# Block-sparse attention into a GELU MLP: the first batch in two units instead of three, with GpSimd gathering for the first

## The chip, the cores and the metric

One core of a Trainium2 chip. The metric is the device time of one execution in microseconds (us), as the median of several runs. Engines in the rows of the profile: PE (TensorE matmul), PEld (TensorE weight load), DVE (VectorE), ACT (ScalarE), POOL (GpSimd), SP (SyncE, which here issues DMAs only). A suffix q is an engine's instruction queue.

## The reference

Attention over 768 positions in 24 blocks of 32, in which a block of queries sees its neighbours, the first and the last block and three drawn blocks; the first and last block of queries see everything. The result goes through a two-layer MLP with an exact GELU.

```python
batch, n_heads, seq, head_dim = (4, 8, 768, 64)      # blocks of 32, 3 drawn per block
scores = scale * np.matmul(q, k.transpose(0, 1, 3, 2))
mask = np.abs(blk_i - blk_j) <= 1
mask = mask | (blk_i == 0) | (blk_j == 0) | (blk_i == n_blocks - 1) | (blk_j == n_blocks - 1)
for qb in range(n_blocks):
    for kb in sampled_blocks[qb]:
        mask[qb * block:(qb + 1) * block, kb * block:(kb + 1) * block] = True
scores = np.where(mask, scores, -1000000000.0)
attn = softmax(scores)
x = np.matmul(attn, v)  # heads side by side: 3072 x 512
h = x @ w_in            # 512 x 2048
out = (0.5 * h * (1.0 + erf(h * inv_sqrt2))) @ w_out   # 2048 x 512
```

## The kernel before

Work is cut into **units**. A unit is a batch and a list of "quads", a quad being four blocks of queries (128 tokens). Each batch has a dense part (query blocks 0 and 23, which see all keys) that goes with its first unit, and 22 sparse blocks. Batches 1 to 3 have two units: quads (1, 2, 0) with the dense part, eleven sparse blocks, and quads (3, 4, 5), eleven more. Batch 0 has three: quad 1 with the dense part (four sparse blocks), quads 2 and 0 (seven), and quads 3, 4, 5 (eleven).

`attention` works through a unit's **rounds**: four dense rounds (`d`), then sparse rounds of two blocks (`s`). A round is `scores` (TensorE), `maxima` (VectorE), `exponentials` (ScalarE, line 347 sparse, 351 dense), `turned` (a VectorE transpose, 364 sparse, 369 dense); a group of rounds (a quad) then has `values` (TensorE, 389 dense, 425 sparse), `divided` (VectorE, 440 to 444) and `outputs` (transposes on TensorE at 454, copies on ScalarE at 462 into `xT`). Rounds are software-pipelined by one. The order of all instructions on an engine is written out by hand: `due` says after which round a group is weighed, `hooks` runs extra work after a round, `quota` says how many matmuls of the previous unit's FFN2 (`ffn2_pieces`, line 497) go between rounds. After a unit's attention come its eight FFN1 steps (`ffn1_step`, line 475, GELU at 478), 64 matmuls whose width is 128 columns per quad; a unit's FFN2 fills the attention of the next.

A sparse block's keys and values are gathered into a buffer `gb`: the neighbours, first and last block by `gather_fixed` (VectorE, lines 252 to 259), the three drawn ones by `gather` (line 268), one copy for each drawn block at a place that is read from a register. `block_numbers` (line 208) loads these registers from a list `vf`. VectorE gathers for most blocks and GpSimd for the rest. For batch 0 keys (128 columns) and values (260 columns) are gathered apart, since k arrives before v.

GpSimd issues all loads, in the order of its queue: k, q, v of batch 0, then the four parts of w_in (line 139) and of w_out (144). A load reuses a semaphore of the eighth load before it and waits for that one. `hold_loads` (line 150) is a one-element GpSimd copy that makes the loads behind it wait for some datum. k and q of batch 0 are transposed on TensorE (`turn_heads`, 219) and placed by ScalarE (225, 228); the keys land in `k0`. Those of later batches are loaded by token (111) and transposed by DMA transposes issued on SP (`turn_keys` 118, `turn_queries` 121), and VectorE scales the keys into place (`place_keys`, 125, in `next_keys`). `turn_queries(1)` writes the space of `k0`, so `k0` is first copied to `kvs[0]` (GpSimd, 657). In the first unit batch 1's loads follow its first GELU output; `next_keys(1)` runs in the third unit's attention.

Of the kernel before, what the change touches and what calls it, by code (L numbers as in the profile page):

```python
# [19 lines left out]
def kernel(  # L20
# [142 lines left out]
    load_kq(kn, k, HALVES[0])  # L163
    load_kq(kn, k, HALVES[1])
    zero = const.tile([P, 1], BF16, name="zero")
# [11 lines left out]
    for h in range(H):  # L177
        load_v(0, h)


# [50 lines left out]
    def spaces():  # L231

        views = [psT.tile([P, PI, PP], BF16, name="pt", tag="T")]
        two = psV.tile([P, 2, 1024], BF16, name="pq", tag="V")
        views += [two[:, i, 0:S].rearrange("p (i c) -> p i c", i=PI) for i in range(2)]
        return views + [psO.tile([P, PI, PP], BF16, name="pt", tag="op")]

# [34 lines left out]
    class Unit:  # L272
        def __init__(self, b, quads, dense, i0=0):
# [3 lines left out]
            self.place = {j: i for i, j in enumerate(sorted(self.js), i0)}  # L277
# [243 lines left out]

    def attention(unit, filler, quota, tail, held=0, hooks=None, late=False, ahead=None):

# [3 lines left out]
        rounds = [(unit, rnd) for rnd in unit.rounds[done:]]  # L527
        due = [(max(e - done + 1 + half, held), grp, half) for e, grp in sorted(unit.ends.items())
               for half in range(2)]
        if ahead:  # L530
# [65 lines left out]
    DVE, POOL = mybir.EngineType.DVE, mybir.EngineType.Pool  # L596
    J0, J1 = sorted(units[3].js), units[2].js
    value_list()
    known = block_numbers(units[0].js, DVE)
    first = [psA.tile([P, 2, 1024], BF16, name="pk", tag="A") for _ in range(2)]  # L600
    first = [x[:, i, 0:S].rearrange("p (i c) -> p i c", i=PI) for x in first for i in range(2)]
    first += spaces()
    for i, (which, pr) in enumerate([(w, pr) for w in "kq" for pr in range(NPR)]):
        turn_heads(which, pr, first[i])
        place_heads(which, pr, first[i])
# [10 lines left out]
    def second_values():  # L616

        nc.gpsimd.tensor_copy(mark, sampled(units[0].place[units[0].js[-1]], NR - 1)[0:1, BW - 1:BW])
        gather(units[1], J0[7:], others, KC, BW, nc.gpsimd)
        ones(1)  # L620
# [3 lines left out]
    QUOTAS = {0: ([4, 10, 2, 0, 0], (0, 0, 0)), 1: ([6, 6, 4, 7, 1, 3, 0, 0, 0], (5,))}  # L624

    def more_numbers(js):
        def load():
            for c in range(0, len(js), 6):
                known.update(block_numbers(js[c:c + 6], DVE))
        return load  # L630

# [4 lines left out]
    for n, unit in enumerate(units):  # L636
# [3 lines left out]
        if nxt is not None and not fresh:  # L640
            gather_fixed(k0 if n == 0 else keys(b), nxt.place)
            if n == 0:
                known |= block_numbers(J0[:3], DVE)
                gather(nxt, J0[:3], known, 0, KC)
                gather(nxt, J0[:3], known, KC, BW)
            elif n == 1:
                gather(nxt, J1[:7], known)
            else:
                gather(nxt, J1[:8], known)
        for s in range(KOUT // 2):  # L650
            ffn1_step(n, 2 * s)
            if s == 0:
                if n == 0:
# [3 lines left out]
                    nc.gpsimd.tensor_copy(kvs[0][:, :, 0:KC], k0)  # L657
                    others |= block_numbers(J1[7:], POOL)
                    gather(units[2], J1[7:], others, engine=nc.gpsimd)
                    turn_keys()  # L660
                    turn_queries(1)
                elif fresh and b + 2 < B:
                    xT, t0 = column[b, unit.groups[-2][0]]
                    hold_loads(xT[0:1, 0, t0:t0 + 1])
                    load_by_token(qn, q, b + 2)
                    load_by_token(kn, k, b + 2)
                    turn_queries(b + 2)
                elif nxt is not None and not fresh:
                    if b + 1 < B:
                        if n > 1:  # L670
                            turn_keys()
# [3 lines left out]
                    if n > 1:  # L675
                        gather(nxt, J1[8:], others, engine=nc.gpsimd)
            if s == 7 and nxt is not None:
                table(AF.Exp)
                if n > 1 and not fresh and b + 1 < B:
                    next_keys(b + 1)  # L680
# [7 lines left out]
        if nxt is None:  # L688
            last_output(n)
        elif n == 0:  # L690
            attention(nxt, filler, *QUOTAS[n], hooks={0: [more_numbers(J1[:8])]})
        elif n == 1:
            attention(nxt, filler, *QUOTAS[n], ahead=units[3], hooks={
                0: [more_numbers(J0[7:9])], 1: [lambda: next_keys(1)]})
# [36 lines left out]
```

## Time and profile before

| | before |
|---|---|
| runs, us | 297.98, 301.18, 304.46 (median 301.18) |
| profiled execution, us | 300.21, span 298.4 |
| granted TensorE clock, mean | 0.983 |
| PE / DVE / ACT / POOL busy, us | 254.5 / 212.9 / 208.3 / 113.8 |
| first, second, third FFN1 start, us | 34.84, 56.33, 84.17 |
| first FFN1 of batch 1 and the one after it, us | 117.69, 147.65 |
| loads of batch 1's k start, us | 36.90 |

A row of a timeline or a chain reads: start, busy time, engine, line, operation, output and inputs, shape, count; in brackets the idle time before it and what ended that. The busy time of a group is a sum over its instructions, which may lie apart or overlap. A row of stretches is headed by start:end and gives busy times by engine in that stretch.

### The profile page before, as it was taken

Reading aid. Unit: us, or ns where it says so; the run is one execution under the profiler, and the core shown is the slowest. Engines: PE = TensorE matmul, PEld = TensorE weight load, DVE = VectorE, ACT = ScalarE, POOL = GpSimd, SP = SyncE. Lnnn points to the kernel's source line nnn. Section 1 sums busy time; section 2 is a strip of 40 time slices with the busy share of each in tenths; the row PEclk is TensorE's granted clock in tenths of the full one; section 3 lists DMA queues with packets and bytes.
Section 4 is the critical chain, followed back from the end, with each engine's and each line's share of the span. In section 5 each row is a group of like instructions: output and inputs, shape, how many; then the busy total and the mean of one; then the engine's idle time right before and its main releaser. Section 6 shows DMA issues by size and latency. Waiting matters only on the chain.

```text
span 298.4 us, 11282 instructions
## 1 busy us (share of the span) xinstructions
PE 254.5 (85%) x4775; PEld 147.6 (49%) x4824; DVE 212.9 (71%) x505; ACT 208.3 (70%) x383; POOL 113.8 (38%) x195
## 2 busy tenths in 40 slices
PE   1655795898699799989998899989998999899994
PEld 0523563574455455635553555545554556355644
DVE  7388576689998886769897959588948979682000
ACT  8677277278786885698767966797768856985611
POOL 8747779970089100890396003930030005000000
PEclk9999998599999999999999999999999999999999
DMA  7999999999059911991099215991000110011002
GB/s 105 158 77 202 207 189 158 169 165 66 4 66 153 138 40 47 160 83 46 32 144 167 81 40 117 102 68 41 37 0 2 40 61 16 2 62 50 0 35 75
DMA packets 90630, 25.39 MB, mean 85 GB/s; under 512 B 81745, under 2 KB 87634, under 8 KB 90578
## 3 DMA queue, kind: packets, MB, share of 16 engines
q0 software_dynamic: 68352, 13.64, 81.9%
q1 hardware_dynamic: 22226, 11.01, 15.1%
q8 instruction: 38, 0.62, 0.9%
q14 instruction: 14, 0.11, 0.1%
HBM read 27.26 MB, written 6.29 MB: 112 GB/s over the span
## 4 chain that ended last, share of the span: by engine, by line
PE 57%; ACT 17%; DVE 11%; DMA 7%; issue 4%; DVEq 2%; POOL 1%; POOLq 0%; ACTq 0%
PE hp L475 25%; PE op L497 13%; PE av L425 11%; ACT pp L347 6%; ACT L375 4%; DMA kv<-in_v_dram 4%; DVE nm L330 3%; ACT g L478 3%; DMA qn<-in_q_dram 3%; DVE pT L364 2%; PE tx L454 2%; PE sc L305 2%; PE av L518 2%; PE op L518 2%; DVE xh L444 2%
## 5 line engine op out<-in xcount | busy, mean ns | idle before, releaser
L475 PE MATMUL hp<-xT,w_in_sb 128*128 128x384 bf16 (+2 forms) x576 | 89.0, 318 | 1.7 <-ACT xT L462 1.3
L347 ACT ACTIVATE pp<-sc,nm 128x256 bf16<-128x256 f32 x176 | 75.1, 542 | 9.5 <-DVE nm L330 9.0
L497 PE MATMUL op<-w_out_sb,g 128*128 128x512 bf16 x288 | 75.8, 380 | 4.8 <-issue 3.7
L478 ACT ACTIVATE g<-hp 128x768 bf16<-128x768 f32 (+4 forms) x81 | 53.6, 675 | 34.1 <-PE hp L475 34.0
L475 PEld LDWEIGHTS <-w_in_sb 128*128 128x128 bf16 x576 | 56.6, 103 | 34.5 <-issue 4.1
L330 DVE TENSOR_REDUCE nm<-sc 128x4 f32<-128x1024 f32 (+1 forms) x48 | 53.0, 1110 | 8.3 <-PE sc L305 8.2
L268 DVE COPY gb<-kv 128x388 bf16 (+1 forms) x195 | 45.9, 318 | 0.9 <-issue 0.8
L497 PEld LDWEIGHTS <-g 128*128 128x128 bf16 x336 | 28.3, 97 | 35.2 <-issue 11.4
L268 POOL COPY gb<-kv 128x388 bf16 (+1 forms) x69 | 31.6, 510 | 24.6 <-DVE gb L259 24.2
L425 PEld LDWEIGHTS <-pT 64*32 64x32 bf16 (+1 forms) x2400 | 27.3, 95 | 24.0 <-DVE pT L364 11.9
L364 DVE STREAM_TRANSPOSE pT<-pp 128x512 f32<-128x512 f32 (+1 forms) x48 | 31.5, 656 | 6.5 <-ACT pp L347 4.6
L425 PE MATMUL av<-kv,pT 64*32 64x130 bf16 (+1 forms) x1344 | 29.6, 228 | 7.5 <-DVE pT L364 4.4
L305 PE MATMUL sc<-gb,qT 64*32 64x256 bf16 x704 | 20.0, 280 | 8.7 <-ACT pp L347 4.2
L133 POOL DMA_DIRECT2D kv<-in_v_dram x32 | 25.6, 807 | 1.7 <-DMA qn<-in_q_dram 1.1
L462 ACT COPY xT<-tx 128x192 bf16<-128x192 bf16 (+2 forms) x33 | 13.6, 441 | 17.1 <-PE tx L454 17.1
L305 PEld LDWEIGHTS <-qT 64*32 64x32 bf16 x832 | 11.6, 90 | 26.8 <-issue 20.6
L375 ACT ACT_TABLE_LOAD x17 | 21.8, 1283 | 0.3
L351 ACT ACTIVATE pp<-sc,nm 128x768 bf16<-128x768 f32 x16 | 17.1, 1101 | 6.7 <-DVE nm L333 6.4
L150 POOL COPY mark<-g 1x1 bf16<-1x1 bf16 x4 | 4.1, 1037 | 45.3 <-ACT g L478 45.3
L425 PE MATMUL av<-gb,pT 64*32 64x130 bf16 x1056 | 20.8, 230 | 0.2 <-issue 0.2
L333 DVE TENSOR_REDUCE nm<-sc 128x1 f32<-128x768 f32 x16 | 15.1, 947 | 7.1 <-PE sc L305 6.9
L444 DVE TENSOR_TENSOR xh<-av,rec 128x512 bf16<-128x512 f32 (+2 forms) x28 | 18.3, 652 | 1.0
(65 smaller groups left out, 216.9 us busy)
## 6 DMA issues: line engine op xcount, KB each, us to landing
out_dram<-os SPq DMA_DIRECT2D x23, 256.0 KB, 2.2
kv<-in_v_dram POOLq DMA_DIRECT2D x32, 96.0 KB, 7.0
kn<-in_k_dram POOLq DMA_DIRECT2D x18, 128.0 KB, 5.9
qn<-in_q_dram POOLq DMA_DIRECT2D x18, 128.0 KB, 5.7
w_in_sb<-in_moe_w_in_dram POOLq DMA_DIRECT2D x4, 512.0 KB, 13.4
w_out_sb<-in_moe_w_out_dram POOLq DMA_DIRECT2D x4, 512.0 KB, 17.4
kn<-in_k_dram POOLq DMA_DIRECT2D x2, 384.0 KB, 5.5
qn<-in_q_dram POOLq DMA_DIRECT2D x2, 384.0 KB, 6.9
```

Of the source, the lines that this page charges most:

```text
L133: nc.gpsimd.dma_start(out=kvs[b % 2][32 * hh:32 * hh + 32, 0:NB, c0:c0 + D], in_=v[b, h].rearrange("(n p) d -> p n d", p=BL))
L268: (engine or nc.vector).tensor_copy(sampled(unit.place[j], r)[:, None, c0:c1], src[:, bass.ds(at[j][r], 1), :])
L305: nc.tensor.matmul(o, lhsT=qT[rows, j // 4, pr, BL * (j % 4):BL * (j % 4) + BL], rhs=rhs(rows, pr), start=True, stop=True)
L330: nc.vector.tensor_reduce(out=nm[:, 0:2 * n].rearrange("p (g j) -> p g j", g=2), in_=A4[:, :, 0:n, :], op=ALU.max, axis=AX.X, negate=True)
L347: nc.scalar.activation(at[:, x // n, x % n], A[:, a:a + 256].rearrange("p (e c k) -> p e c k", e=2, k=BL), AF.Exp, bias=nm[:, x:x + 1])
L364: nc.vector.transpose(pt.rearrange("p g c x -> p (g c) x")[:, :, 64 * s:64 * (s + n)].bitcast(F32), pp[:, 0:512 * n].bitcast(F32).rearrang ...
L375: nc.scalar.activation(junk, zero[0:1, 0:1], func)
L425: nc.tensor.matmul(av[32 * s:32 * (s + w), h, V2 * G:V2 * G + V2], lhsT=pv[rows, c % 4, BL * s:BL * (s + w), c // 4], rhs=src[rows], start ...
L444: nc.vector.tensor_tensor(xh[rows, :, 0:m * D].rearrange("p h (x d) -> p h x d", d=D), a[:, :, :, 0:D], rec[rows, :, 0:m, None].to_broadca ...
L475: nc.tensor.matmul(hp[:, i, 0:T], lhsT=w_in_sb[:, ki, (m + i) * P:(m + i + 1) * P], rhs=xTs[n % 2][:, ki, 0:T], start=(ki == 0), stop=(ki ...
L478: nc.scalar.activation(g[:, m + i[0]:m + i[1], 0:T], hp[:, i[0]:i[1], 0:T], AF.Gelu)
L497: nc.tensor.matmul(op, lhsT=g[:, m, t * P:(t + 1) * P], rhs=w_out_sb[:, m, :], start=(m == 0), stop=(m == KOUT - 1))
```

## The change

Batch 0 has two units like the others, so the first unit has four dense rounds and six sparse rounds (eleven blocks) ahead of the first FFN1, which is then 384 columns wide.

- VectorE gathers the keys of the first quad only. GpSimd gathers the keys of the other two quads (21 copies, between its w_in loads) and the values of all three (33 copies, from hooks after rounds 4, 6 and 8), with the w_out loads between them. An explicit list `order` says after which rounds the groups are weighed.
- VectorE loads four lists of block numbers at the start instead of one, GpSimd three.
- `gather_fixed` runs by quad: once at the start, then after rounds 0 and 2.
- The spare blocks of `kvs[1]` are zeroed partly by GpSimd (six of 25), and its ones are written ahead of the weight loads.
- The transposes of k and q go to PSUM tiles that alternate over four pools.
- `k0` is copied to `kvs[0]` by VectorE after the first unit's attention.
- Batch 1's k and q loads still follow the first GELU output, which is now that of the wider first unit; GpSimd's share of the second unit's gather and then batch 1's v follow them. `next_keys(1)` runs after round 2 of the second unit's attention.

```diff
-    nc.scalar.copy(kvs[1][:, :, KC:BW], zero[:, :, None].to_broadcast([P, NB + 1, BW - KC]))
+    nc.scalar.copy(kvs[1][:, 0:FILLED, KC:BW], zero[:, :, None].to_broadcast([P, FILLED, BW - KC]))
...
+    nc.gpsimd.memset(kvs[1][:, FILLED:NB + 1, KC:BW], 0.0)
+    ones(1)
...
-    units = [Unit(0, (1,), True, 9), Unit(0, (2, 0), False), Unit(0, (3, 4, 5), False)]
-    units += [Unit(b, quads, dense) for b in range(1, B)
-              for quads, dense in (((1, 2, 0), True), ((3, 4, 5), False))]
+    units = [Unit(b, quads, dense) for b in range(B)
+             for quads, dense in (((1, 2, 0), True), ((3, 4, 5), False))]
...
-    known = block_numbers(units[0].js, DVE)
+    known = block_numbers(J0[:9], DVE) | block_numbers(J1[:8], DVE)
...
-    gather(units[0], units[0].js, known, 0, KC)
-    gather_fixed(k0, units[0].place)
-    for part in range(4):
-        load_w_in(part)
-    for part in range(4):
-        load_w_out(part)
-    others = block_numbers(J0[7:], POOL)
-    gather(units[1], J0[7:], others, 0, KC, nc.gpsimd)
...
-    attention(units[0], iter(()), [0] * 7, (0, 0, 0), 5,
-              {4: [lambda: gather(units[0], units[0].js, known, KC, BW)], 5: [second_values]})
+    gather(units[0], grps[0], known, 0, KC)
+
+    def fixed(t):
+        gather_fixed(k0, {j: units[0].place[j] for j in grps[t]})
+    fixed(0)
+    others = block_numbers(J0, POOL) | block_numbers(J1[8:], POOL)
+    load_w_in(0)
+    hold_loads(gb[0:1, GW * 2 - KC:GW * 2 - KC + 1])
+    gather(units[0], grps[1], others, 0, KC, nc.gpsimd)
+    load_w_in(1)
+    gather(units[0], grps[2], others, 0, KC, nc.gpsimd)
+    load_w_in(2)
+    load_w_in(3)
+
+    def values_of(t, *parts):
+
+        def ask():
+            gather(units[0], grps[t], others, KC, BW, nc.gpsimd)
+            for part in parts:
+                load_w_out(part)
+        return ask
+    attention(units[0], iter(()), [0] * 11, (0, 0, 0), (5, 6, 7, 7, 9, 9, 10, 10),
+              {0: [lambda: fixed(1)], 2: [lambda: fixed(2)], 4: [values_of(0, 0)],
+               6: [values_of(1, 1)], 8: [values_of(2, 2, 3)]})
...
             if n == 0:
-                known |= block_numbers(J0[:3], DVE)
-                gather(nxt, J0[:3], known, 0, KC)
-                gather(nxt, J0[:3], known, KC, BW)
-            elif n == 1:
-                gather(nxt, J1[:7], known)
-            else:
-                gather(nxt, J1[:8], known)
+                nc.vector.tensor_copy(kvs[0][:, :, 0:KC], k0)
+            gather_fixed(keys(b), nxt.place)
+            gather(nxt, J1[:8], known)
...
                     hold_loads(g[0:1, 0, 0:1])
                     load_by_token(kn, k, 1)
                     load_by_token(qn, q, 1)
-                    nc.gpsimd.tensor_copy(kvs[0][:, :, 0:KC], k0)
-                    others |= block_numbers(J1[7:], POOL)
-                    gather(units[2], J1[7:], others, engine=nc.gpsimd)
+                    gather(nxt, J1[8:], others, engine=nc.gpsimd)
+                    for h in range(H):
+                        load_v(1, h)
                     turn_keys()
                     turn_queries(1)
...
-            attention(nxt, filler, [3, 11, 2, 5, 3, 8, 1, 7, 1], (5,), ahead=units[n + 2])
+            attention(nxt, filler, [3, 11, 2, 5, 3, 8, 1, 7, 1], (5,), ahead=units[n + 2],
+                      hooks={} if n else {2: [lambda: next_keys(1)]})
```

More of the change, by code (lines that the diff above doesn't have):

```diff
@@ L520, in last_output, with attention @@
             store(n, quad, cols, op)
-    def attention(unit, filler, quota, tail, held=0, hooks=None, late=False, ahead=None):
+    def attention(unit, filler, quota, tail, order=None, hooks=None, late=False, ahead=None):
         done = begun.pop(unit, 0)
         rounds = [(unit, rnd) for rnd in unit.rounds[done:]]
-        due = [(max(e - done + 1 + half, held), grp, half) for e, grp in sorted(unit.ends.items())
-               for half in range(2)]
+        due = [(e - done + 1 + half, grp, half) for e, grp in sorted(unit.ends.items()) for half in range(2)]
+        if order:
+            due = [(at, grp, half) for at, (_, grp, half) in zip(order, due)]
         if ahead:
@@ L596 @@
     DVE, POOL = mybir.EngineType.DVE, mybir.EngineType.Pool
-    J0, J1 = sorted(units[3].js), units[2].js
+    J0, J1 = sorted(units[0].js), sorted(units[1].js)
+    grps = units[0].groups
     value_list()
-    known = block_numbers(units[0].js, DVE)
[L600 to L605, printed above, removed]
@@ L621 @@
-    attention(units[0], iter(()), [0] * 7, (0, 0, 0), 5,
-              {4: [lambda: gather(units[0], units[0].js, known, KC, BW)], 5: [second_values]})
[L624 to L630, printed above, removed]
+    known = block_numbers(J0[:9], DVE) | block_numbers(J1[:8], DVE)
+    for (which, pr), bank in zip([(w, pr) for w in "kq" for pr in range(NPR)], spaces()):
+        turn_heads(which, pr, bank)
+        place_heads(which, pr, bank)
@@ L689 @@
             last_output(n)
[L690 to L694, printed above, removed]
         elif fresh:
```

31 lines of the change are left out of this document (16 added, 15 removed).

## The prediction

> **What bounds the kernel now.** I read the chain that ended last first, then the busy time by stretch, cut at the starts of the first, third and fourth FFN1 (columns: stretch, its length, then PE, PEld, DVE, ACT and POOL busy with instruction counts, the granted TensorE clock, DMA share, GB/s).
>
> ```profile
> PE 57%; ACT 17%; DVE 11%; DMA 7%; issue 4%; DVEq 2%; POOL 1%; POOLq 0%; ACTq 0%
> ...
> 117.69:147.65 29.96, 28.37 (x524) 15.39 (x529) 24.30 (x59) 22.46 (x43) 14.14 (x20) 1.00 1.26 82
> 34.84:84.17 49.33, 40.12 (x846) 26.10 (x852) 39.44 (x95) 33.23 (x72) 27.05 (x38) 0.90 1.55 124
> 84.17:298.40 214.23, 197.51 (x3531) 109.96 (x3573) 150.57 (x348) 152.27 (x285) 61.99 (x92) 1.00 0.69 66
> 0.00:34.84 34.84, 16.85 (x398) 11.54 (x399) 22.93 (x65) 22.75 (x28) 24.75 (x67) 1.00 2.00 146
> ```
>
> From 84.17 on TensorE is busy 92% of the time; nothing there is edited. All that the change can move lies before 84.17, where the FFN1 of batch 0's last unit starts: an opening of 34.84 in which TensorE is idle for half of the time, and 49.33 in which two small units are finished and the third unit's attention is done. The same pair of stages for a full unit (FFN1 of three quads, then the attention of a (3,4,5) unit) is the row 117.69:147.65: 29.96 us. So the question is when the new first FFN1 can start; call that X. The next one then starts at X + 29.96 plus any new wait W, and the new time is 300.21 - 84.17 + X + 29.96 + W. The profiled execution took 300.21 for a span of 298.4; 1.8 lie around it and stay. It is 1.0 below the median of the three runs, 301.18, and inside their spread of 298 to 304.5.
>
> **What is saved.** The timeline of the FFN1 matmuls (start, busy, engine):
>
> ```profile
> 34.84 5.95 PE L475 MATMUL hp<-xT,w_in_sb 128*128 128x128 bf16 x64 [0.46 <-ACT xT L462]
> ...
> 56.33 8.71 PE L475 MATMUL hp<-xT,w_in_sb 128*128 128x256 bf16 x64 [0.41 <-ACT xT L462]
> ...
> 117.69 10.56 PE L475 MATMUL hp<-xT,w_in_sb 128*128 128x384 bf16 x64
> ```
>
> Two passes of 14.66 become one of 10.56, and one round of attention tail, table loads and restart goes. Against it stands a first FFN1 that waits for eleven blocks instead of four. Without new waits X would break even at 84.17 - 29.96 = 54.2.
>
> **X: the opening on GpSimd.** All value copies and the keys of groups 2 and 3 now go through GpSimd's queue, behind its DMA issues. Rows:
>
> ```profile
> 3.30 0.20 POOL masks.py:197 MEMSET identity<- 128x128 bf16 x1
> ...
> 12.37 0.76 POOL L133 DMA_DIRECT2D kv<-in_v_dram  x1 [1.09 <-DMA qn<-in_q_dram]
> ...
> 25.14 2.78 PE L389 MATMUL av<-kv,ptd 64*64 64x130 bf16 x93 [0.89 <-DMA kv<-in_v_dram]
> 25.29 0.74 POOL L144 DMA_DIRECT2D w_out_sb<-in_moe_w_out_dram  x1 [0.52 <-DVE nm L330]
> ...
> 26.60 2.91 POOL L268 COPY gb<-qT 128x128 bf16 x12 [0.56 <-issue]
> 29.44 0.18 POOL L618 COPY mark<-gb 1x1 bf16<-1x1 bf16 x1
> 29.57 4.16 POOL L268 COPY gb<-kv 128x260 bf16 x12
> 33.67 1.44 POOL L156 MEMSET kv<- 32x24 bf16 x8
> ...
> 49.50 2.87 POOL L657 COPY kv<-qT 128x3200 bf16<-128x3200 bf16 x1
> ```
> ```profile
> L208 DVEq TENSOR_LOAD <-vf x5: 818/1433/2178, 7.1 to 67.2; - x5
> L208 POOLq TENSOR_LOAD <-vf x2: 1024/1886/2749, 25.3 to 48.7; - x2
> ```
>
> In the changed kernel's instruction order GpSimd does, after its last load of V (12.37 + 0.76 = 13.13): the memset of six spare value blocks, 1560 elements wide. No row has one: it lies between 0.20 (the 128-wide memset) and 1.40 (half of the 3200-wide copy); it is nearer to the long row, so 1.40. Then the ones moved up from line 620, 1.44: 15.97. Three loads of block numbers instead of one; rows span 0.82 to 2.75, where the longest ran beside a copy; I take 1.02 each: 19.0. w_in part 0, 0.75, and the mark, 0.18: 20.0. Keys of group 2, 12 copies at (29.44 - 26.60)/12 = 0.24: 22.8. w_in part 1: 23.6. Keys of group 3, nine: 25.7. w_in parts 2 and 3: 27.2. Call this P. The new mark waits for VectorE's fixed blocks, which are written by about 16, before GpSimd reaches it; the value copies also wait for TensorE's scores of their own group, for the first group done at 24 by my count of rounds. V itself landed at 25.1, so P cannot be under that; with a cheap memset and loads of 0.82 it is 25.4, with loads of 1.43 it is 28.4.
>
> From P the queue is values (33.67 - 29.57 = 4.10), w_out part 0 (0.74), values (4.10), part 1 (0.74), values of three blocks (nine copies, 3.08): P + 12.76 = 40.0. Behind that stands the last group's weighing. The chain of waits shows the two kinds of groups:
>
> ```profile
> 48.31 1.88 PE av L425 x101
> ...
> 51.74 1.92 PE av L425 x90
> ```
>
> The three-block group took 1.92 up to 53.66, and its FFN1 began at 56.33: 2.67 for division, transposes and copies. X = 40.0 + 0.1 + 1.92 + 2.67 = 44.7, between 42.9 and 45.9 by the bounds of P.
>
> VectorE does not come later than that. It starts its keys when k0 is whole:
>
> ```profile
> 12.59 0.20 DVE L239 COPY qT<-qT 128x128 bf16<-128x128 bf16 x1 [5.50 <-ACT qT L225]
> ...
> 16.31 1.82 DVE L333 TENSOR_REDUCE nm<-sc 128x1 f32<-128x768 f32 x2 [0.33 <-PE sc L305]
> ```
>
> Its four loads of numbers instead of one fit into the 5.50 of idle time (four at 1.1, ending at 11.5; at 1.43 they would end at 12.8). The transposed heads now alternate over separate PSUM tiles and ScalarE's zero fill is a quarter shorter, so k0 can only be earlier: a gain of 0 to 1.5 at 12.59 that I count as nothing, because GpSimd's queue decides X. Two more sets of fixed blocks cost VectorE at most 3.4 (12.59 to 15.98 holds one set and a group of copies); by my count of reductions and transposes it has done the last transpose at 39.8, just ahead of GpSimd's 40.0. If GpSimd were quicker, this count would hold X at about 44.
>
> The weights move behind the key copies: w_in part 3 is issued at 27 instead of 19.5 and is wanted 17 us later; w_out parts 2 and 3 are issued around 41 and wanted at X + 10.6. Both are covered.
>
> **W: the next batch's keys.** The loads of batch 1 were asked for at 36.90, 33 us ahead of their use; now they hang on the new first FFN1, while VectorE's next_keys stands only two rounds into the following attention.
>
> ```profile
> 36.40 0.18 POOL L150 COPY mark<-g 1x1 bf16<-1x1 bf16 x1 [1.29 <-ACT g L478]
> 36.90 5.28 POOL L111 DMA_DIRECT2D kn<-in_k_dram  x6 [0.31 <-PE hp L475]
> ...
> 119.19 0.81 ACT L478 ACTIVATE g<-hp 128x768 bf16<-128x768 f32 x1 [0.84 <-PE hp L475]
> ```
> ```profile
> kn<-in_k_dram POOLq DMA_DIRECT2D x18, 128.0 KB, 5.9
> ```
> ```profile
> 50.17 5.26 SPq L118 DMA_TRANSPOSE ptd<-kn  x1
> ...
> DMA to landing us min/median/max: 5.5/6.2/8.9
> ```
> ```profile
> 70.60 1.15 DVE L125 TENSOR_SCALAR kv<-ptd 128x768 bf16<-128x768 bf16 x4
> ...
> 71.78 0.20 DVE L239 COPY kv<-kv 128x128 bf16<-128x128 bf16 x1
> ...
> 125.19 1.62 DVE L125 TENSOR_SCALAR kv<-ptd 128x768 bf16<-128x768 bf16 x4 [1.59 <-DMA ptd<-kn]
> ...
> 135.90 0.71 DVE L364 STREAM_TRANSPOSE pT<-pp 128x512 f32<-128x512 f32 x1
> ```
>
> The first g of a full unit is written at 119.19 + 0.81 - 117.69 = 2.3 after its FFN1 starts; the first key load follows 0.55 later (X + 2.9), the sixth 4.4 after that, and lands 5.9 later: X + 13.2. The DMA transpose then runs beside the query loads, as at 50.17, where it took the 8.9 of the third row; the 6.2 and 5.5 are those with less traffic. I take 8.9: X + 22.1, with X + 19.4 as the other end. VectorE reaches next_keys where the steady attention starts its third sparse transpose, 135.90 - 117.69 = X + 18.2. So it waits 3.9 (other end 1.2), and the five instructions of 1.35 now lie in the rounds too. Behind them on VectorE stand the transposes and maxima of all further rounds, and ScalarE and TensorE wait for those. That VectorE can wait at this line shows in the 1.59 of the row at 125.19. W = 5.25, between 2.5 and 5.25.
>
> **Covered.** GpSimd's copy of k0 goes to VectorE, ahead of the 24 gathers under the first FFN1:
>
> ```profile
> 85.37 0.56 DVE L257 COPY gb<-kv 128x1536 bf16<-128x1536 bf16 x1
> ...
> 86.85 7.97 DVE L268 COPY gb<-kv 128x388 bf16 x27
> ...
> 119.43 4.17 DVE L268 COPY gb<-kv 128x388 bf16 x24
> ```
>
> Twice 0.56 for the copy (2.87 at most, GpSimd's time), fixed blocks about 2.8, and 24 gathers at 7.97/27 (beside DMA issues on GpSimd) make 11.0, from X - 1.5 on: done about X + 9.5, under an FFN1 of 10.56; uncovered it would cost 1 to 2. GpSimd's nine copies end at about X + 18, when round five asks for them. V of batch 1 is issued by X + 24, over 13 us ahead of its first reader.
>
> **Sum.** 300.21 - 84.17 + 44.7 + 29.96 + 5.25 = 295.95, say 296.0: 4.2 less than the profiled execution.
>
> **The rivals.** *Keys in time.* The transpose lands like the undisturbed ones (W 2.5): 293.2; with P at its lower end (X limited to 44 by VectorE or 42.9) 291.5 to 292.5. For it: two of three transposes took 5.5 and 6.2. Against: those had no loads beside them.
>
> *The clock falls.* TensorE now idles some 5 us in the wait W and several times 2 us before X. The row before the fall and the two in it:
>
> ```profile
> 44.00:48.00 4.00, 2.15 (x30) 1.00 2.43 156
> 48.00:52.00 4.00, 2.37 (x124) 0.66 2.47 159
> 52.00:56.00 4.00, 2.85 (x98) 0.50 1.58 162
> ```
>
> A stretch of half busy was followed here by about ten us at half clock. If that falls on a first FFN1 or the stage after W, which are 95% TensorE, half of ten us is lost: 301.0, no gain. Against it: the opening, where TensorE was busy for 16.85 of 34.84, kept a clock of 1.00. The Trainium skill, "TensorE: Matmul & The Clock Gate", section "What's actually happening", says that an idle window of about 3.4 us halves the clock and a busy one restores it; by that the wait W would always bring the fall, and the sum would be 301. The opening's clock of 1.00 does not agree with it.
>
> *GpSimd's copies slow down.* They now run beside VectorE at its busiest. The slowest copy of the trace against the median:
>
> ```profile
> L268 POOL COPY gb<-kv x69: 391/510/871, 29.6 to 250.1; 128x388 bf16 x57, 128x260 bf16 x12
> ```
>
> The 54 copies on the path to X cost 21 x 0.24 + 33 x 0.34 = 16.3. At 871/510 of that they add 11.5: 307.5, slower. It decides from 1.26 times the rows on, where the gain of 4.2 is gone. Against: most copies ran near 0.5 beside a busy VectorE.
>
> **How the numbers follow.** Forecast 0.42 (its own range 293.5 to 298.5), keys in time 0.30, clock 0.14, slow copies 0.14. Two per cent of the median is 6.0, about what this kernel's runs can tell from no change: faster is below 295.2, slower above 307.2. Faster: 0.28 of the second case and 0.14 of the forecast's lower side, 0.42. Slower: the heavy half of the copies, 0.08. The rest 0.50. The range runs from 290.0, below the early keys, to 303.0, past the clock case; what lies outside is most of the slow copies.
>
> **What would show it.** A first 384-wide FFN1 at 43 to 46, with the last value copies on GpSimd at about 40 right ahead; VectorE idle 1 to 4 us before line 125 with the key transpose as releaser; the second FFN1 at about 80. Wrong: X past 50, an X set by VectorE, no wait at line 125, or a granted clock of 0.5 after X.

## The result, and the profile after

The changed kernel takes 315.38 us (median of four runs, 314.68 to 316.42), the kernel before 301.74 beside it (four runs, 297.98 to 304.46): a ratio of 1.050, interval 1.039 to 1.060, slower. The forecast was 296.0. The profiled execution took 314.98 for a span of 312.6. Some executions of every version run slower, at a lower granted clock: the ratios leave out those more than 1.5% above the fastest of their version, while the times are medians of all, and the traces of "v later" (308.95), of the first trial of "TensorE kept busy" (313.61), of "and aligned loads" (301.50) and of "the same again" (300.76) are of such executions.

The same stretches as before, cut at the starts of the first and second FFN1 (columns: length, busy time of PE, PEld, DVE, ACT and POOL with counts, granted clock, DMA share, GB/s):

```profile
0.00:52.22 52.22, 23.73 (x659) 15.13 (x659) 32.51 (x74) 28.60 (x44) 35.49 (x99) 0.89 1.47 126
52.22:100.01 47.79, 33.50 (x528) 16.85 (x528) 27.75 (x62) 21.85 (x42) 21.16 (x32) 0.80 1.68 97
100.01:312.60 212.59, 203.08 (x3575) 109.91 (x3573) 151.19 (x348) 151.79 (x285) 61.99 (x91) 1.00 0.71 67
```

The long last stretch is 1.6 shorter than before. Everything lost lies ahead of the second FFN1, which starts at 100.01 instead of 84.17 (+15.8) and was forecast for 79.9. Along the steps of the forecast, those 20.1 us divide so:

| | forecast | measured | late by |
|---|---|---|---|
| P, GpSimd's first value copy | 27.2 | 32.03 | 4.8 |
| from P to the first FFN1 | 17.5 | 20.2 | 2.7 |
| length of the first FFN1 | 10.56 | 13.05 | 2.5 |
| from its end to the second FFN1 | 24.65 | 34.74 | 10.1 |

*P.* The timeline of GpSimd in the opening (start, busy time, idle time before it and what ended that):

```profile
13.10 1.40 POOL L180 MEMSET kv<- 128x1560 bf16 x1
14.56 1.30 POOL L156 MEMSET kv<- 32x24 bf16 x8
24.01 0.77 POOL L139 DMA_DIRECT2D w_in_sb<-in_moe_w_in_dram  x1 [8.15 <-issue]
...
32.03 4.19 POOL L276 COPY gb<-kv 128x260 bf16 x12
...
41.79 3.16 POOL L276 COPY gb<-kv 128x260 bf16 x9
```

The memset is the forecast 1.40, and from the first copy to the end of the last, 32.03 to 44.95, it takes 12.9 (forecast 12.76). What is wrong is the 8.15 of idle time at 24.01: GpSimd's queue is loading block numbers into registers. The groups of the loads show it (count: min/median/max in ns, first and last start), and the chain that ended last shows VectorE's four at the head of the opening, where they hold its first key copy to 16.20 (the last row below, from VectorE's timeline):

```profile
L211 DVEq TENSOR_LOAD <-vf x4: 521/1518/5204, 7.1 to 15.6; - x4
L211 POOLq TENSOR_LOAD <-vf x3: 826/2492/5124, 14.9 to 22.6; - x3
```
```profile
7.12 5.20 DVEq L211
12.41 1.21 DVEq L211
13.69 1.82 DVEq L211
15.59 0.52 DVEq L211
...
16.20 0.20 DVE L247 COPY qT<-qT 128x128 bf16<-128x128 bf16 x1 [9.11 <-issue]
```

The table follows the forecast's path, through GpSimd. The chain that ended last reaches the first FFN1 another way: it goes through these four loads, VectorE's copies and maxima and the weighings on TensorE, and none of GpSimd's copies is on it. So the 4.8 of P is not what held the first FFN1 in this run; more on this under "Fewer numbers at the start".

*From P to the first FFN1, and its length.* The timeline of TensorE and the clock by stretch:

```profile
37.74 0.30 PE L435 MATMUL av<-kv,pT 64*32 64x130 bf16 x15 [0.71 <-issue]
...
43.39 0.26 PE L435 MATMUL av<-kv,pT 64*32 64x130 bf16 x1 [1.66 <-issue]
...
49.04 0.62 PE L435 MATMUL av<-kv,pT 64*32 64x130 bf16 x21 [1.25 <-issue]
...
52.22 13.05 PE L485 MATMUL hp<-xT,w_in_sb 128*128 128x384 bf16 x64 [0.41 <-ACT xT L472]
```
```profile
48.00:52.00 4.00, 2.10 (x53) 1.50 (x53) 1.80 (x4) 0.73 (x2) 0.00 (x0) 0.50 1.21 192
56.00:60.00 4.00, 4.00 (x22) 2.28 (x21) 4.00 (x16) 1.62 (x2) 3.74 (x6) 0.84 0.70 45
```

TensorE stops three times inside a group of matmuls that waits for nothing ("issue"), for 0.71, 1.66 and 1.25, and the granted clock is 0.50 from 40 until the FFN1 has run for some five us.

*To the second FFN1.* Loads, DMA transposes and those who wait for them, then the time from issue to landing of the two transposes and a wait of SyncE's queue:

```profile
56.38 5.30 POOL L111 DMA_DIRECT2D kn<-in_k_dram  x6 [0.26 <-issue]
...
65.37 6.59 SPq L118 DMA_TRANSPOSE ptd<-kn  x1
...
70.92 4.99 POOL L133 DMA_DIRECT2D kv<-in_v_dram  x7
...
76.69 10.32 SPq L121 DMA_TRANSPOSE qT<-qn  x1
...
78.89 1.17 DVE L125 TENSOR_SCALAR kv<-ptd 128x768 bf16<-128x768 bf16 x4 [6.05 <-DMA ptd<-kn]
...
83.73 0.85 PE L435 MATMUL av<-kv,pT 64*128 64x130 bf16 x28 [6.68 <-DVE pT L374]
...
91.80 0.83 PE L315 MATMUL sc<-kv,qT 64*32 64x512 bf16 x8 [6.89 <-DMA qT<-qn]
```
```profile
ptd<-kn SPq DMA_TRANSPOSE x1, 13.5
qT<-qn SPq DMA_TRANSPOSE x1, 15.1
...
SPq L121 <- DMA qn<-in_q_dram: 4.5, 1, 4.5
```

The keys land when forecast: their transpose starts at 65.37, which is X + 13.15. It then takes 13.5, not 8.9; VectorE waits 6.05 for it at line 125, and TensorE 6.68 for the transpose that VectorE does behind that. The queries' transpose waits for the loads of q (the last row) and starts at 76.69, while the keys' is still under way; it takes 15.1 beside the loads of V, and TensorE waits 6.89 for it: a second wait, which the forecast does not have.

### The profile page after: what moved, and what is told of

Read it like the earlier page. It is cut to its first block, busy times and chain, and to the rows that moved or that the text cites. A ratio compares the mean times of both kernels' runs of the same rounds, so it can differ in the third digit from the quotient of the medians.

```text
span 312.6 us, 11185 instructions
## 1 busy us (share of the span) xinstructions
PE 260.3 (83%) x4760; PEld 141.9 (45%) x4760; DVE 211.4 (68%) x481; ACT 202.2 (65%) x369; POOL 118.6 (38%) x221
## 4 chain that ended last, share of the span: by engine, by line
PE 60%; ACT 15%; DVE 10%; DMA 8%; issue 3%; DVEq 3%; ACTq 0%
PE hp L485 25%; PE op L507 15%; PE av L435 11%; ACT pp L357 6%; DMA qT<-qn 5%; ACT L385 4%; DMA ptd<-kn 4%; PE sc L315 3%; DVEq L211 3%; ACT g L488 2%; PE tx L464 2%; PE av L528 2%; PE op L528 2%; DVE nm L340 1%; DVE nm L343 1%
## 5 line engine op out<-in xcount | busy, mean ns | idle before, releaser
L485 PE MATMUL hp<-xT,w_in_sb 128*128 128x384 bf16 x512 | 87.5, 333 | 0.8 <-ACT xT L472 0.4
L507 PE MATMUL op<-w_out_sb,g 128*128 128x512 bf16 x336 | 86.2, 382 | 0.1
L488 ACT ACTIVATE g<-hp 128x768 bf16<-128x768 f32 (+1 forms) x72 | 52.1, 738 | 33.9 <-PE hp L485 33.9
L485 PEld LDWEIGHTS <-w_in_sb 128*128 128x128 bf16 x512 | 50.9, 99 | 37.7 <-issue 5.9
L276 POOL COPY gb<-kv 128x388 bf16 (+1 forms) x87 | 36.6, 476 | 24.5 <-DVE gb L267 24.1
L276 DVE COPY gb<-kv 128x388 bf16 x177 | 42.6, 320 | 0.2
L435 PE MATMUL av<-kv,pT 64*32 64x130 bf16 (+1 forms) x1344 | 30.5, 231 | 13.1 <-DVE pT L374 8.2
L472 ACT COPY xT<-tx 128x512 bf16<-128x512 bf16 (+1 forms) x32 | 13.6, 450 | 27.1 <-PE tx L464 26.9
L315 PE MATMUL sc<-gb,qT 64*32 64x256 bf16 x704 | 20.1, 289 | 11.6 <-ACT pp L357 7.0
L150 POOL COPY mark<-g 1x1 bf16<-1x1 bf16 x3 | 7.2, 2394 | 52.3 <-ACT g L488 52.3
L343 DVE TENSOR_REDUCE nm<-sc 128x1 f32<-128x768 f32 x16 | 15.0, 945 | 13.7 <-PE sc L315 13.2
L133 POOL DMA_DIRECT2D kv<-in_v_dram x32 | 22.9, 731 | 2.1 <-DMA qn<-in_q_dram 2.1
```

The costliest lines, as they stand in the source:

```text
L133: nc.gpsimd.dma_start(out=kvs[b % 2][32 * hh:32 * hh + 32, 0:NB, c0:c0 + D], in_=v[b, h].rearrange("(n p) d -> p n d", p=BL))
L276: (engine or nc.vector).tensor_copy(sampled(unit.place[j], r)[:, None, c0:c1], src[:, bass.ds(at[j][r], 1), :])
L315: nc.tensor.matmul(o, lhsT=qT[rows, j // 4, pr, BL * (j % 4):BL * (j % 4) + BL], rhs=rhs(rows, pr), start=True, stop=True)
L435: nc.tensor.matmul(av[32 * s:32 * (s + w), h, V2 * G:V2 * G + V2], lhsT=pv[rows, c % 4, BL * s:BL * (s + w), c // 4], rhs=src[rows], start ...
L485: nc.tensor.matmul(hp[:, i, 0:T], lhsT=w_in_sb[:, ki, (m + i) * P:(m + i + 1) * P], rhs=xTs[n % 2][:, ki, 0:T], start=(ki == 0), stop=(ki ...
L488: nc.scalar.activation(g[:, m + i[0]:m + i[1], 0:T], hp[:, i[0]:i[1], 0:T], AF.Gelu)
```

## Experiments

Each edit is made to the changed kernel unless another is named. Where the expectations name theories by letters, A says that the loads of k and q come too late, B that the loads of v beside the transposes slow them, E that a register load's cost hangs on where its list starts.

**k and q earlier.** The loads of batch 1's k and q go right behind the last w_out loads, without a hold.

```diff
-                    hold_loads(g[0:1, 0, 0:1])
-                    load_by_token(kn, k, 1)
-                    load_by_token(qn, q, 1)
...
+    def next_loads():
+        load_by_token(kn, k, 1)
+        load_by_token(qn, q, 1)
...
-               ... 8: [values_of(2, 2, 3)]})
+               ... 8: [values_of(2, 2, 3), next_loads]})
```

> The changed kernel, but batch 1's k and q are loaded right behind the last w_out part, without waiting for the first GELU output (about 10 us earlier). Theory A (the second unit's attention is held by the next batch's keys and queries because they are asked for late): VectorE's wait at line 125 falls from 6.1 to under 1.5 and TensorE's wait for the queries from 6.9 to under 3; first FFN1 start unchanged at 52; the second starts at about 90 instead of 100; time 304 to 306. Rival (the DMA transposes take 13 to 15 us whatever the start, and the stall only moves): the two waits keep more than 8 us in sum, time above 311.

Measured: 305.63 (four runs), ratio to before 1.018, interval 1.010 to 1.025. The second FFN1 starts at 90.86, 9.2 sooner. Neither line 125 nor the scores wait for a transpose any more, though the queries' still took 15.8: it is only early enough. One stop grew, in the middle of a weighing:

```profile
77.47 0.34 PE L435 MATMUL av<-gb,pT 64*32 64x130 bf16 x14
81.92 0.40 PE L435 MATMUL av<-gb,pT 64*32 64x130 bf16 x10 [4.11 <-issue]
```

So the waits of 6.05 and 6.89 hang on the late loads: with early ones both are gone. A part of what they gave back went into this stop.

**v later.** k and q stay late; v's loads are held until the queries' transpose has landed.

```diff
-                    for h in range(H):
-                        load_v(1, h)
                     turn_keys()
                     turn_queries(1)
+                    hold_loads(qTs[1][0:1, 0, 0, 0:1])
+                    for h in range(H):
+                        load_v(1, h)
```

> The changed kernel, but batch 1's v loads wait until the query transpose has landed. Theory B (the small packets of v stretch the two DMA transposes): key transpose 13.5 to about 9, query transpose 15.1 to about 8, both waits together fall from 13 to about 4; v then arrives late for the second FFN1's gathers and gives back 2 to 4; time 306 to 310. Rival (the transposes wait on the query loads or on each other): their times stay above 12, time 315 or more.

Measured: 305.13, ratio 1.014 (1.006 to 1.022); second FFN1 at 91.58.

```profile
ptd<-kn SPq DMA_TRANSPOSE x1, 11.4
qT<-qn SPq DMA_TRANSPOSE x1, 5.5
```

With v out of the way the queries' transpose falls from 15.1 to 5.5. The keys' falls only from 13.5 to 11.4; the query loads still run beside it, as the queries' transpose starts at 76.40, when the last of them has landed. The same step from early k and q to early k and q with late v (below) takes the queries' transpose from 15.8 to 5.8 and the keys' from 11.4 to 8.8. So loads beside a DMA transpose cost up to 10 us of it here, and the forecast's 8.9 was not the upper end.

**Fewer numbers at the start.** VectorE loads 21 numbers ahead of its first copies instead of 51, GpSimd 33 instead of 42; the rest later.

```diff
-    known = block_numbers(J0[:9], DVE) | block_numbers(J1[:8], DVE)
+    known = block_numbers(J0[:7], DVE)
-    others = block_numbers(J0, POOL) | block_numbers(J1[8:], POOL)
+    others = block_numbers(J0, POOL)
... (and the lists left out here loaded later, by hooks and under the first FFN1)
```

> The changed kernel, but VectorE loads 21 block numbers at the start instead of 51 (the others after rounds of the first and second unit), and GpSimd 33 instead of 42 (the last nine ahead of their use). Theory C (a register load costs 0.18 to 0.19 us for each number): VectorE's first key copy moves from 16.2 to 11.0, GpSimd's first w_in issue from 24.0 to 22.3, the first FFN1 from 52.2 to 49.5 to 51, since GpSimd's values still decide; time 312 to 314. Rival (the first load was slow for another reason, its count does not matter): VectorE's first copy stays at 14 or later.

Measured: 311.17, ratio 1.036 (1.027 to 1.044); first FFN1 at 48.84, second at 96.82.

```profile
12.21 0.20 DVE L247 COPY qT<-qT 128x128 bf16<-128x128 bf16 x1 [5.10 <-ACT qT L231]
...
32.45 4.20 POOL L276 COPY gb<-kv 128x260 bf16 x12
...
36.01 0.98 PE L435 MATMUL av<-gb,pT 64*32 64x130 bf16 x18 [0.75 <-POOL gb L276]
```

VectorE starts its copies at 12.21, not at the 11.0 of the expectation, and GpSimd's first w_in load stays at 24.40. P is 32.45, no earlier than in the changed kernel, and still the first FFN1 comes 3.4 sooner; now TensorE waits for GpSimd's copies inside the first weighing (four waits, 2.7 together). So GpSimd's queue, with P at 32, would have let the first FFN1 start by 48.8, and the rest up to 52.22 came from the other side of the chain, VectorE and TensorE: VectorE's four loads, and the stops of TensorE, which are absent from the weighings of this trace. This run does not tell these two apart.

The single load of 21 numbers took 4.97: the count of numbers does not give the cost by itself. Against it, in the changed kernel 22 numbers from place 36 of the list took 1.82 and 22 from place 3 took 5.20. That led to the next experiment.

**Loads that start on a multiple of four numbers (16 bytes).** A load begins at the multiple of four at or before its first number and takes 20 at most.

```diff
-        for c0 in range(js[0] * NR, (js[-1] + 1) * NR, 22):
-            c1 = min(c0 + 22, (js[-1] + 1) * NR)
+        start = js[0] * NR // 4 * 4
+        for c0 in range(start, (js[-1] + 1) * NR, 20):
+            c1 = min(c0 + 20, (js[-1] + 1) * NR)
...
+        vals = vals[js[0] * NR - start:]
```

> The changed kernel, but every register load starts at a multiple of four numbers (16 bytes) of the list and takes 20 instead of 22 at once; VectorE then loads 54 numbers at the start, GpSimd 45. Theory E (a load that starts off a 16-byte boundary costs 0.23 us for each number, one on it 0.09): VectorE's first key copy moves from 16.2 to about 12, GpSimd's first w_in issue from 24.0 to about 20, P from 32 to 28, the first FFN1 from 52.2 to 47 to 49; time 310 to 312. Rival (cost by the count alone, 0.18 us each): VectorE's copy at 16.5 or later, GpSimd's issue at 24.5, time 315 to 316.

```profile
L212 DVEq TENSOR_LOAD <-vf x4: 351/1214/1587, 7.1 to 11.4; - x4
L212 POOLq TENSOR_LOAD <-vf x3: 836/1052/1502, 14.9 to 17.6; - x3
```
```profile
18.98 0.89 POOL L139 DMA_DIRECT2D w_in_sb<-in_moe_w_in_dram  x1 [2.94 <-issue]
...
27.20 4.21 POOL L278 COPY gb<-kv 128x260 bf16 x12
...
47.17 12.03 PE L487 MATMUL hp<-xT,w_in_sb 128*128 128x384 bf16 x64 [0.41 <-ACT xT L474]
```

The longest load falls from 5.2 to 1.6, as many loads as before, a few numbers more. P is 27.20, which is the forecast's 27.2. The first FFN1 comes 5.05 sooner, but the time only falls to 312.09, ratio 1.028 (1.017 to 1.039): the second starts at 95.93, as TensorE's wait for the queries grows from 6.89 to 8.51. Why it grows is not shown: the two transposes take 12.6 and 15.2, about as in the changed kernel.

The same edit in the kernel before, as a control:

> The kernel before with register loads that start at a multiple of four numbers and take at most 20 at once; nothing else changed. Theory: the cost per number depends on where the load starts, in this kernel too: the load of 18 numbers that starts one past a boundary (2.7 us beside a copy) and those of nine and six fall to about 0.09 us a number, 0.8 to 1.8 each. None lies on the path before 84.17 for more than 1 us, so the time stays within 1 us of before (ratio 0.995 to 1.0). Rival: the loads' cost comes from the work beside them; they stay at 1.4 to 2.7.

```profile
L209 DVEq TENSOR_LOAD <-vf x5: 594/855/1585, 7.1 to 64.9; - x5
L209 POOLq TENSOR_LOAD <-vf x2: 1018/1056/1094, 23.7 to 47.7; - x2
```

The loads that began off a multiple of four fall: nine numbers from place 3 from 2.18 to 0.86 and six from place 54 from 1.43 to 0.59 on VectorE, twelve from place 57 (not 18, as the expectation has it) from 2.75 to 1.09 on GpSimd. Those that began on one keep their time: 18 numbers from place 36 took 1.58 and take 1.59. The time is 300.21 against 300.60, ratio 0.999 (0.996 to 1.003): no difference. In the kernel before, the faster loads gain nothing; the change made them matter.

**TensorE kept busy.** 21 matmuls of 512 columns, whose result nobody reads (`busy`, its body left out here), fill TensorE's idle places from round 6 on.

```diff
-    attention(units[0], iter(()), [0] * 11, (0, 0, 0), (5,
+    attention(units[0], busy(21), [0] * 6 + [2, 2, 3, 5, 4], (0, 0, 5), (5,
```

> The changed kernel with 21 extra matmuls of 512 columns into a PSUM bank that nobody reads, in TensorE's gaps between 35 and 52. Theory D (the clock fell to half from 40 to 57 because TensorE was idle in the window before): the granted clock stays at 1.0 through the first FFN1, which takes 10.6 instead of 13.05; it starts 0 to 1.5 earlier; time 311 to 313. Rival (the clock does not follow TensorE's own activity): the half clock stays and the extra matmuls make it 316 to 319.

The clock by stretch of this kernel:

```profile
44.00:48.00 4.00, 3.56 (x141) 1.97 (x140) 1.92 (x5) 1.78 (x6) 3.32 (x8) 1.00 0.96 137
48.00:52.00 4.00, 2.12 (x67) 1.30 (x67) 1.16 (x4) 2.00 (x3) 0.00 (x0) 0.80 1.13 181
```

Full clock lasts ten us longer, until a stop of 2.10 ("issue") at 47.7; then it falls again, and the FFN1, which starts 2.8 later at 54.99, takes 11.64. The time, 313.5 (308.2 to 317.0), can't be told from the 315.38 of the changed kernel. The second trial starts from the best version (the last one below) and puts 30 such matmuls into the idle places from 15 us on:

> The best version so far (aligned loads, early k and q, late v, the first quad's values on VectorE) with 30 matmuls of 512 columns whose result nobody reads, put into TensorE's idle places from 15 us on (3.4 before the first scores, 2.0 and 0.8 after, 4.5 before the fourth dense round, then two behind each round). Theory of the clock: TensorE is at half clock through the opening because it is mostly idle; with 30 x 0.43 = 13 us more work from 15 on it is at full clock by about 30, the 313 ns weighings become about 215, the first FFN1 takes 10.6 to 11 us instead of 12.9 and the time falls to 293 to 296 (from 297.5). Rival: the idle places are too long for the filler, or the stops of TensorE's own queue break the activity; the clock falls again before the first FFN1, which still takes over 12, and the time is 297 to 300.

```profile
48.88 10.56 PE L487 MATMUL hp<-xT,w_in_sb 128*128 128x384 bf16 x64 [0.41 <-ACT xT L474]
```

Now the first FFN1 takes 10.56, as in the steady part of the kernel before, instead of 12.5 to 12.9. So its extra length is the clock, and the clock follows TensorE's activity. The time does not fall: it is 301.41, above what the theory (293 to 296) and its rival (297 to 300) gave, with a ratio to before of 0.999 (0.995 to 1.003), where the version without the extra matmuls has 0.988 beside it. They delay the FFN1's start by 1.3 to 2.1 (47.56 and 46.82 in the two traces without them, 48.88 with them), so that it ends no earlier than the 59.3 of the second of these, and the loads behind it shift as well: the keys' transpose takes 11.8 instead of 8.9, and line 125 waits 3.38 again.

**Where TensorE stops without a releaser.** In the trace of the early-k-and-q version the stops of 2.48, 1.53 and 4.11 come after 478, 606 and 988 weight loads of the program. A weight load and its matmul are two instructions, so these lie a multiple of 256 instructions apart, 128 and 382 weight loads (the last within two). The three stops of the changed kernel come after 350, 478 and 606, in the same steps. In the trace of the early-k-and-q version a transfer of 16 KB in the queue of kind "instruction" ends 1.4 to 1.5 us ahead of the end of each of the three stops. 64 one-column matmuls early in this version move all later work by 128 instructions:

```diff
-    attention(units[0], iter(()), [0] * 11, (0, 0, 0), (5,
+    attention(units[0], tiny(64), [16, 16, 32, 0, 0, 0, 0, 0, 0, 0, 0], (0, 0, 0), (5,
... (`tiny`, the one-column matmuls, left out here)
```

> The early-k-and-q version with 64 one-column matmuls (128 TensorE instructions with their weight loads) put into the idle places of the first three rounds, so that everything behind them stands 128 instructions later in TensorE's program. Theory of the program fetch: the stops with no releaser (2.48 at instruction 961, 1.53 at 1217 and 4.11 at 1985 of that version, all 193 past a multiple of 256) come where a block of 256 instructions ends and the next has not arrived; they move 128 instructions of the work forward, to what was at 833, 1089 and 1857, and stand again at 193 past a multiple of 256; the place of the 4.11 stop (the 129th instruction before it and after) runs through. Rival: the stops belong to the work at these places (PSUM, the data, the traffic beside them); they stay at the same matmuls, now 65 past a multiple of 256. The time is within 3 us of 305.

```profile
47.94 0.43 PE L435 MATMUL av<-gb,pT 64*32 64x130 bf16 x11
50.20 0.41 PE L435 MATMUL av<-gb,pT 64*32 64x130 bf16 x13 [1.84 <-issue]
...
79.01 0.37 PE L435 MATMUL av<-gb,pT 64*32 64x130 bf16 x18
84.49 0.30 PE L435 MATMUL av<-gb,pT 64*32 64x130 bf16 x6 [5.11 <-issue]
```

The stops come after 478, 606 and 989 weight loads again (0.63, 1.84 and 5.11), now in other pieces of work: a group of 24 is cut 11 and 13, another 18 and 6 where it was 14 and 10. They belong to the place in the program, not to the work. The one-column matmuls cost more than I had reckoned (0.22 each), so the first FFN1 came at 56.26 and the time was 311.8 in its one run, 3.8 over the expectation's upper end.

**The repairs together.** Early k and q with late v; then with the aligned loads; then also with the first quad's values copied by VectorE instead of GpSimd:

```diff
-               ... 4: [values_of(0, 0)],
+               ... 4: [lambda: gather(units[0], grps[0], known, KC, BW), lambda: load_w_out(0)],
```

> The changed kernel with batch 1's k and q loaded right behind the last w_out part and its v held until the query transpose has landed. Theories A and B together: first FFN1 unchanged at 52, no wait at line 125, none for the queries, the second FFN1 at 85 to 88 instead of 100; time 300 to 303. Rival (what is left of the stall in kq_early, a 4.1 us stop of TensorE in the midst of a group's weighing, has another cause than v's packets): the stop stays, the second FFN1 at 90, time 305.

> The changed kernel with aligned register loads, early k and q of batch 1 and held v. If the three terms add: first FFN1 at 47 to 49, second at 80 to 84, time 295 to 299, level with or ahead of the kernel before. Rival (the wait moves on: v of batch 1 lands too late for the second FFN1's gathers): a wait of VectorE for v behind the second FFN1, time 300 or more.

> As the run before it, and the first quad's values are copied by VectorE instead of GpSimd. If GpSimd's queue sets the first FFN1: it starts 2 to 4 earlier than without, time 293 to 297. Rival (VectorE and TensorE set it): the start moves later by up to 2.4, VectorE's twelve copies, time 297 to 301.

> The best version so far once more, beside the one with the 30 extra matmuls and with more runs: 297.5, ratio to before 0.98 to 0.99, first FFN1 at 47.6 taking 12.9, second at 83.5.

| | first FFN1 | second FFN1 | time | ratio to before |
|---|---|---|---|---|
| changed kernel | 52.22 | 100.01 | 315.38 | 1.050 (1.039 to 1.060) |
| early k and q, late v | 52.48 | 87.43 | 302.72 | 1.003 (0.998 to 1.008) |
| and aligned loads | 48.38 | 83.86 | 299.15 | 0.992 (0.987 to 0.996) |
| and first values on VectorE | 47.56 | 83.47 | 297.48 | 0.983 (0.971 to 0.994) |
| the same again | 46.82 | 82.53 | 298.88 | 0.988 (0.981 to 0.995) |

The last version is faster than both kernels, by 1.2 to 1.7% against the kernel before, which is under two per cent but clear of 1.000 in both measurements. In its second trace GpSimd waits for TensorE ahead of its value copies, so its queue no longer sets X, and neither line 125 nor the scores wait for a transpose:

```profile
31.00 4.21 POOL L278 COPY gb<-kv 128x260 bf16 x12 [3.24 <-PE sc L317]
...
46.82 12.48 PE L487 MATMUL hp<-xT,w_in_sb 128*128 128x384 bf16 x64 [0.41 <-ACT xT L474]
...
79.58 0.24 PE L437 MATMUL av<-gb,pT 64*32 64x130 bf16 x4 [2.71 <-issue]
```

The second FFN1 starts at 82.53. Against the forecast's 79.9 there are the 1.9 of the half-clock FFN1, this stop of 2.71 and an X of 46.8 instead of 44.7, less the 5.25 of W, which did not come; 1.1 stay unexplained.

## Why the prediction was wrong

What happened is none of the rivals alone: the slow outcome had been left to slow copies on GpSimd, and those did not come. Two of the four signs of being wrong that were named came plainly, X past 50 (52.22) and a granted clock of 0.5 after X, and a third, an X set by VectorE, is what the chain shows.

*The saving* came in part. Two passes became one, but the stage behind X, once its waits are gone, is 35.0 to 35.9 in the repaired versions instead of 29.96. A longer first FFN1 and a program stop are 4.0 to 4.7 of the difference, and about 1 is not explained.

*P, the term that was mis-sized first.* Memset, ones, weight loads, 21 key and 33 value copies came out close to the sum (54 copies: 16.5 against 16.3, so the rival of slow copies is refuted). The three register loads on GpSimd were taken at 1.02 each and measured 5.12, 2.49 and 0.83; the four on VectorE, "fit into the 5.50 of idle time", took 8.75 together. I priced a load by the piece from rows between 0.82 and 2.75 and put the long ones down to a copy beside them. The rows of the kernel before had the answer, had I set each beside its list: nine numbers from place 3 took 2.18 and twelve from 57 took 2.75, but 18 from 36 took 1.58 and twelve from 24 took 1.02. In the changed kernel the cost is again about 0.24 us a number off a multiple of four (22 from 3: 5.20; 11 from 25: 2.49; 5 from 25: 1.21) and 0.08 to 0.09 on one (22 from 36: 1.82; 9 from 60: 0.83). The aligned loads brought P to 27.20. The Trainium skill, "Runtime: NRT & Kernel Launch", section "Instruction fetch mechanics", gives some 200 ns a register, where it budgets the register loads that the runtime puts in; by that, as an estimate, the 51 and 42 numbers cost 10.2 and 8.4 us. The measured 8.75 and 8.44 are near it, but as a mean: no load here costs 0.20 a number, the slow ones take 0.23 to 0.26 and the fast ones of the changed kernel 0.08 to 0.09. The estimate would have told of the loss, though not of how to avoid it.

*"VectorE does not come later than that."* This step failed as well, and by the chain it is the one that set X. With its first key copy at 12.59 VectorE was to hold X at about 44. The four loads put that copy at 16.20, 3.6 later, and the three stops of TensorE on the chain add 3.6: 51.2 of the measured 52.22. Through GpSimd, with P at 32.45, the first FFN1 came at 48.84. Aligned loads repair both sides at once, so no run shows what GpSimd's loads cost by themselves.

*From P to X.* GpSimd's 12.9 held. From its last copy to the FFN1 it took 7.3 instead of 4.7: the last weighing starts 1.4 after that copy, since it waits for VectorE's division of the group before, which had a stop of 1.66, and it holds a stop of 1.25 itself. The half clock is not the reason here, for the 1.92 of the forecast was taken at half clock too (0.50 in 52:56 of the kernel before). That kernel's chain has a small stop as well, 0.39 of "issue" at 53.98, inside the 2.67 that I took for division, transposes and copies; I read past it.

*The clock.* This rival was right in kind, and I argued it away on a misread column. The page of the profile gives the opening a granted clock of 1.00, but the first clock record of that trace stands at 39.07, and what the page has ahead of it is no measurement. The matmul rows tell otherwise. The same matmuls of the kernel before in its opening and in a steady stage, and of the second trial with extra matmuls where its recorded clock is 0.50 (32 to 36):

```profile
L389 PE MATMUL av<-kv,ptd x96: 284/312/313, 23.4 to 27.6; 64*64 64x130 bf16 x96
```
```profile
L389 PE MATMUL av<-kv,ptd x96: 214/216/243, 100.9 to 103.3; 64*64 64x130 bf16 x96
```
```profile
L401 PE MATMUL av<-kv,ptd x96: 217/312/314, 32.6 to 36.9; 64*64 64x130 bf16 x96
```

312 ns against 216, and 312 is what half clock gives: the opening ran at half clock in the kernel before. So it did in the changed one up to about 36, where sixteen scores take 0.63 against 0.41 at 65.2. So the rule of the Trainium skill, "TensorE: Matmul & The Clock Gate", section "What's actually happening" (throttled by default and after an idle window, released by sustained work), agrees with the trace, and my sentence against it was wrong. Its price here is the 2.5 of the first FFN1 and some of the stretch behind the wait for the queries (0.64 in 92:96), not the five us that I had given it.

*W, the largest term.* The chain of steps was right up to the landing of the keys (X + 13.15, forecast X + 13.2) and in naming line 125. Two things failed. The transpose of 8.9, taken as the upper value, was 13.5, for q's loads and then v's ran beside it. And the step stopped at the keys: the queries' transpose follows them, behind the last load of q, V's loads fall on it, and TensorE waits for it too. "W between 2.5 and 5.25" became 15.3 (47.79 less the 29.96 and the FFN1's 2.5), of which 13.6 are TensorE's waits of 6.68 and 6.89. Each repair alone brought the second FFN1 forward by 8 to 9 us, and both together by 12.6.

## What to carry to other kernels

When a stage that covers loads is shortened, follow the moved loads through everything that hangs on them, to the last transfer and its reader, not only to the first. Where two engines are forecast to be done within a few us of each other, price both with the same care, for the one that was "not later" may be the one that decides. A queue instruction that the page doesn't count as busy (a register load) has a price per item; where one row is five times another of its kind, find out what differs before taking the median. And check the granted clock against the duration of a matmul of known shape before using it as evidence.

## What the runs showed of the hardware

- A register load costs about 0.24 us a number if its list starts off a multiple of four int32 numbers (16 bytes), on VectorE and on GpSimd. On one, whole fours cost 0.07 to 0.09 a number (20 numbers: 1.35 to 1.59) and the numbers left over about 0.24 each (22 from place 36: 1.82, 20 from there: 1.35). One load does not fit: in the version with fewer numbers at the start six numbers from place 24 took 1.48, in the kernel before 0.82. So the start is not the whole rule.
- TensorE stops, here for up to 5.1 us, at places of its program that lie a multiple of 256 instructions apart; not every such place has a stop. The stops end 1.2 to 2.1 us after a transfer of 16 KB. The page of the profile lists these transfers as a queue of their own, 37 for 4760 weight loads and as many matmuls, one for each 257:

```profile
q8 instruction: 37, 0.61, 0.9%
```

  The stops stayed at their places of the program, and so moved to other work, when 128 instructions were put in ahead. That a late transfer causes them, that short matmuls use up a block faster than the next one comes, and that the loads beside the transfer make it slow, rests on the times alone. No run here shortened the program.
- A DMA transpose of a batch's keys or queries takes 5.5 with no loads beside it, 8.9 beside the query loads of the kernel before, and 11.4 to 15.8 beside more loads.
